# Attention and a channel mixture on one core: unsplit float32 scores for the first five head pairs, GpSimd casts in the early weight conversion, another PSUM half for early scores, a new order

## The chip, the cores and the metric

One core of a Trainium2 chip runs the whole program in one launch. The metric is device time in microseconds (us), lower is better. The profile names the engines PE (TensorE), DVE (VectorE), ACT (ScalarE), POOL (GpSimd) and SP (SyncE, which issues the DMAs).

## What is computed

```python
# q, k, v: (batch 8, heads 8, tokens 576, 64);  x: (8, 576, 512)
scores = q @ k^T / sqrt(64)
scores = where(scores >= max(scores) - tau, scores, -1e9)
attn   = exp(scores - max); attn /= sum(attn) + 1e-9
x      = attn @ v                       # heads side by side: 512 channels
theta  = x @ w_theta
zr, zi = x * cos(theta), x * sin(theta)
y      = w_tok_r @ zr + w_tok_i @ zi    # over the 576 tokens
u      = x + y
out    = u + max(u @ w_ch, 0)
```

## The kernel before, in words

Two heads form a pair; there are 32 pairs, four to a batch element. A pair n has five score units S n.0 to S n.4. A unit of the first four holds 128 query rows of both heads; the fifth holds the last 64 rows of both heads together. `unit` computes a unit's scores into four PSUM banks, DVE reads them out with a running minimum (the eviction, line 780), a small DVE instruction adds the threshold (790), ACT forms the masked exponentials in two passes per head (804, 811), and DVE transposes 32x32 blocks (823, 825). `values` multiplies the transposed weights by v (V n, line 840, in plain float32), and `divide` applies the row sums. When four pairs of a batch element are done, `mixture` does the rest for it: the theta products (T, line 948), sine and cosine on ACT, transposes on PE (1091), the token products (K, 1136) and the products with w_ch (T again).

Products that need more than one pass of the fast PE type (float32r) are split into a high word and a low word, and three products high-high, high-low, low-high are summed. For q and k this is done in `prepare_q` and `prepare_k`: load the raw tile, scale q by the gate (line 696; only from pair 3 on, since for pairs 0 to 2 the eviction multiplies by the gate instead), cast to the high word (705 and 722 on DVE, 707 and 724 on ACT), subtract to get the low word (`low`, line 530, on DVE or POOL).

The weights come as 64-bit floats. `convert` turns a chunk of them into a high and a low float32r word: ACT takes the magnitude (578), POOL or DVE clamps it (583), DVE shifts and merges bits (597, 604, 611), DVE multiplies the low 32 bits by a power of two (`word`, 615), ACT casts the high word (626), PE sums three terms (634 to 636; in the text, C) and ACT writes the low word (640). There are 17 chunks, called turns: 0 to 3 are w_theta (512 columns), 4 to 12 the token weights (576 columns, two C each), 13 to 16 w_ch. C0 to C21 belong to turns 0 to 12.

Nothing is scheduled at run time. The program lists its operations, and two tables decide the rest: `ORDER` says in which order they are issued (each engine works its own part in that order), and `PLACES` says in which buffer or PSUM bank each tile lies. All score units and all value products lie in banks 0 to 3 before the change (the digit 0 of a tile that is four banks wide); banks 4 to 7 serve the rest:

```python
ps = Buf(cl["bank"], lambda b: psum[:, b : b + 2 * len(heads)], psum=True,
         places=(0,) if i < 4 else (0, 2), wide=2 * len(heads))
terms = ((0, 0), (0, 1), (1, 0))
```

Of the kernel before, what the change touches and what calls it, by code (L numbers as in the profile page):

```python
# [64 lines left out]
        "0101201220220101200012012001201201201201022100121010210210012012011200"  # L65
    ),
    "xl": (
        "012102012001010231010120303120123201301230213012310230123301210232013102310232013"
    ),
    "xh": (  # L70
        "01203121013003013120120213201323010103210310230123210301230213012312030123102310231023102320131023"
    ),
    "rb": (
        "010101010001010101010000001000100000011101010100"
    ),
    "bank": (
        "67765674454565747576560000000070000007000000700000074567545744744475677457667547667576477675000000600000"
        "06000000600000056547646757456744754665674747677564570000005000000700000060000004765476576574567747655567"
        "74476545675600000040000007000000600000077564757467556437476556747564674775670000006000000600000070000006"
        "65745576564654776746554766575647745600000040000004000000600000047456567465556774564574677546754765760000"  # L80
        "00300000070000007000000576457675457467357456654767676476547600000060000006000000500005573273654727244354"
        "663726656457766453"
    ),
    "z": (
        "1201010212001200120012001200120012001200101"
    ),
    "rawq": (
        "01011100110010100101101010100010"
    ),
    "q": (  # L90
        "0123012301302103120312031203120312031203120312031201320123012301"
    ),
    "rawk": (
        "00000000000000000000000000000000"
    ),
    "k": (
        "0123012301230123012301230123012301230123012301230123012301230123"
# [5 lines left out]
        "10231032013201230132100231032101023031201230231202031012030112031021012020120123021032110213201230120310"  # L103
        "13202130012303102130120321103201203012302130023103201320120312231020123012313210103202103121032031023102"
        "31010230012301320132030123201301230130210230120301231123021031203121031321020310"
# [7 lines left out]
        "10120210010011201001001102100101002001102012011001001102"  # L113
    ),
    "rows": (
        "00100001001000101001010101000000"
    ),
    "a": (
        "00000000000000000000000000000000"
# [1193 lines left out]
```

## Time and profile before

| | |
|---|---|
| median of 3 runs | 926.42 us (924.15 to 927.21) |
| profiled execution | 924.78 us, of which the span from the first to the last instruction is 923.0 us |
| PE, DVE, ACT, POOL busy over the span | 866.0, 714.4, 699.5, 314.3 us |

PE is busy for most of the span, but its matmuls are pipelined and a busy time includes their fill, so the stretch matters more than the average. The span falls into an opening (up to the first score unit of pair 5, at 128.3 us), in which the five first pairs and the 13 first weight chunks are worked and hardly any mixture, and the rest, in which attention and mixture are interleaved.

### The profile page before, as it was taken

The page shows a single profiled execution, that of the slowest core. Times are in us where ns is not written, and L with a number is a line of the kernel's source. Part 1 is how long each engine was busy: PE and PEld are TensorE (multiplying, and loading weights), DVE is VectorE, ACT ScalarE, POOL GpSimd, SP SyncE. Part 2 cuts the span into 40 slices and gives each one's busy share as a digit, 9 for nine tenths or more (in the row PEclk, how much of TensorE's full clock was granted, in tenths as well). Part 3 has the DMA queues.
Part 4 walks back from the last instruction along what each step waited for, and adds up shares of the span by engine and source line. Part 5 has one row for each costly group of instructions (what it writes and reads, how often), then busy time and mean ns, then how long its engine had stood idle before and what let it go on. Part 6 is the DMA issues. An engine that isn't in the chain of part 4 may idle for free.

```text
span 923.0 us, 34024 instructions
## 1 busy us (share of the span) xinstructions
PE 866.0 (94%) x14632; PEld 779.5 (84%) x14632; DVE 714.4 (77%) x1598; ACT 699.5 (76%) x1406; POOL 314.3 (34%) x390
## 2 busy tenths in 40 slices
PE   4778799999999999999999999998999999999998
PEld 3556688788898988988999989897989989989898
DVE  7998889987787887778877887777975886876443
ACT  5788898865897678965899659976797659975540
POOL 0212451613443244513244343342334442321202
PEclk9988999999999999999999999999999999999999
DMA  7356535355342364024534351434534243423502
GB/s 261 115 161 224 166 138 178 101 167 178 131 158 93 131 209 175 17 80 151 201 103 144 110 187 67 170 107 143 183 129 129 82 146 122 138 83 131 164 22 75
DMA packets 62375, 126.15 MB, mean 137 GB/s; under 512 B 22512, under 2 KB 31632, under 8 KB 58128
## 3 DMA queue, kind: packets, MB, share of 16 engines
q1 hardware_dynamic: 62080, 123.97, 40.2%
q8 instruction: 115, 1.88, 0.8%
q14 instruction: 36, 0.29, 0.1%
q10 hardware_dynamic: 144, 0.00, 0.0%
HBM read 110.17 MB, written 13.78 MB: 134 GB/s over the span
## 4 chain that ended last, share of the span: by engine, by line
PE 64%; DVE 20%; ACT 8%; issue 3%; DMA 3%; POOL 1%; SPq 0%; DVEq 0%; POOLq 0%; ACTq 0%
PE banks_ps__66 L1136 21%; PE banks_ps__66 L840 14%; PE banks_ps__66 L948 13%; PE banks_ps__66 L759 11%; DVE sc L780 7%; DVE a L823 5%; PE banks_ps__66 L1091 3%; ACT sc L804 2%; ACT s L811 2%; DVE nm L790 1%; PE banks_ps__66 L634 1%; DMA z<-in_w_theta_dram 1%; DVE xl L530 1%; DVE z L1016 1%; DVE zl L1116 1%
## 5 line engine op out<-in xcount | busy, mean ns | idle before, releaser
L804 ACT ACTIVATE sc<-sc,nm 128x576 f32<-128x576 f32 x288 | 216.7, 771 | 78.6 <-DVE nm L790 75.1
L811 ACT ACTIVATE s<-sc,small 128x576 f32<-128x576 f32 x288 | 222.9, 775 | 5.1 <-DVE a L823 0.6
L823 DVE STREAM_TRANSPOSE a<-s 128x576 f32<-128x576 f32 x256 | 189.7, 759 | 35.3 <-PE banks_ps__66 L840 28.6
L759 PE MATMUL banks_ps__66<-k,q 64*128 64x288 f32 (+1 forms) x1728 | 178.7, 320 | 32.7 <-DVE sc L780 24.0
L780 DVE TENSOR_SCALAR_CACHE_REDUCE sc<-banks_ps__66 128x576 f32<-128x576 f32 x261 | 186.2, 741 | 13.2 <-PE banks_ps__66 L759 11.5
L759 PEld LDWEIGHTS banks_ps__66<-k,q 64*128 64x128 f32 (+1 forms) x1728 | 141.4, 194 | 61.1 <-DVE sc L780 37.9
L948 PE MATMUL banks_ps__66<-xh,wm 128*128 128x288 f32 x1024 | 168.9, 302 | 4.2 <-issue 1.6
L840 PE MATMUL banks_ps__66<-a,v 32*64 32x144 f32 x9216 | 165.0, 288 | 4.9 <-DVE sc L780 3.9
L1136 PE MATMUL banks_ps__66<-wt_h,zh 128*128 128x288 f32 x576 | 164.4, 309 | 1.7 <-DVE xT L1148 1.2
L840 PEld LDWEIGHTS banks_ps__66<-a,v 32*64 32x64 f32 x9216 | 146.9, 132 | 18.0 <-issue 9.2
L1136 PE MATMUL banks_ps__66<-wt_l,zh 128*128 128x288 f32 x576 | 160.6, 302 | 0.0
L948 PEld LDWEIGHTS banks_ps__66<-xh,wm 128*128 128x128 f32 x1024 | 143.4, 188 | 14.6 <-issue 8.6
L1066 POOL TENSOR_TENSOR z<-z,xT 128x288 f32<-128x288 f32 x112 | 91.7, 850 | 118.9 <-ACT z L1047 96.4
L1136 PEld LDWEIGHTS banks_ps__66<-wt_h,zh 128*128 128x128 f32 x576 | 108.9, 190 | 6.9 <-issue 3.9
L1136 PEld LDWEIGHTS banks_ps__66<-wt_l,zh 128*128 128x128 f32 x576 | 108.6, 189 | 2.8 <-issue 2.6
L530 POOL TENSOR_TENSOR k<-rawk,k 128x288 fp32r<-128x288 f32 x62 | 52.9, 860 | 168.5 <-DVE k L722 93.0
L530 POOL TENSOR_TENSOR xl<-xT,xh 128x288 fp32r<-128x288 f32 x78 | 66.8, 878 | 109.6 <-ACT xh L907 67.6
L1136 PE MATMUL banks_ps__66<-wt_h,zl 128*128 128x288 f32 x576 | 95.8, 301 | 0.0
L948 PE MATMUL banks_ps__66<-xl,wm 128*128 128x288 f32 x512 | 92.6, 300 | 2.9 <-issue 2.7
L1116 DVE TENSOR_TENSOR zl<-banks_ps__66,zh 128x512 fp32r<-128x512 f32 (+1 forms) x96 | 51.9, 547 | 56.1 <-ACT zh L1097 56.0
L1136 PEld LDWEIGHTS banks_ps__66<-wt_h,zl 128*128 128x128 f32 x576 | 81.5, 188 | 2.9 <-issue 2.4
L948 PEld LDWEIGHTS banks_ps__66<-xl,wm 128*128 128x128 f32 x512 | 75.0, 188 | 7.1 <-issue 6.0
(78 smaller groups left out, 996.3 us busy)
## 6 DMA issues: line engine op xcount, KB each, us to landing
v<-in_vp_dram SPq DMA_DIRECT2D x32, 1152.0 KB
wm<-wm_dram SPq DMA_DIRECT2D x64, 512.0 KB
rawq<-in_qT_dram SPq DMA_DIRECT2D x31, 320.0 KB
rawk<-in_kT_dram SPq DMA_DIRECT2D x31, 288.0 KB
out_dram<-xT SPq DMA_DIRECT2D x31, 288.0 KB
rb<-sums_dram SPq DMA_DIRECT2D x64, 128.0 KB
z<-in_w_tok_dram SPq DMA_DIRECT2D x9, 576.0 KB
wm_dram<-rb SPq DMA_DIRECT2D x16, 256.0 KB
```

The costliest lines, as they stand in the source:

```text
L530: eng.tensor_tensor(out=out()[:, c0:c1], in0=in0()[:, c0:c1], in1=in1()[:, c0:c1], op=ALU.subtract)
L759: nc.tensor.matmul(ps()[:, 2 * j + h, :HS], q[a]()[r, i * P : (i + 1) * P], k[c]()[r, h * HS : (h + 1) * HS], start=(x == 0), stop=(x == 2),)
L780: lambda j=j, sc=sc, scaled=scaled: nc.vector.tensor_scalar(out=sc().rearrange("p (a b) -> p a b", a=2), in0=ps()[:, 2 * j : 2 * j + 2, :H ...
L804: lambda j=j, sc=sc: nc.scalar.activation(out=sc(), in_=sc(), func=AF.Prelu, bias=nm()[:, 2 + j : 3 + j], scale=-1.0, alpha=STEEP),
L811: lambda j=j, sc=sc, total=total, weights=weights: nc.scalar.activation(out=weights(), in_=keys(sc()), func=AF.Exp, bias=back, accum_out=p ...
L823: nc.vector.transpose(out=a()[:, :, j, 32 * i : 32 * i + 32], in_=src.rearrange("p (c q) -> p c q", q=32))
L840: nc.tensor.matmul(ps()[64 * h : 64 * h + 64, b, :w], v()[r, c, h, :], a()[r, c, h, :], start=(c == 0), stop=(c == 17))
L948: nc.tensor.matmul(ps[h]()[:, :HS], wm()[:, a, c, :], parts[c][bb]()[:, h * HS : (h + 1) * HS], start=first and n == 0, stop=final and n = ...
L1066: eng.tensor_tensor(out=zi, in0=zi, in1=x[m]()[:, c0:c1], op=ALU.mult)
L1091: nc.tensor.transpose(out=tp()[:, i * P : (i + 1) * P], in_=z()[:, c : c + P], identity=ident)
L1116: lambda zh=zh, zl=zl, tv=tv: nc.vector.tensor_tensor(out=zl(), in0=tv(), in1=zh().bitcast(F32), op=ALU.subtract),
L1136: nc.tensor.matmul(ps()[:, :HS], zz[c][lo]()[:, zz[c][2]], w[:, c, hs], start=(q + n == 0), stop=(q + n == len(work) - 1),)
```

## The change

- For pairs 0 to 4 (`WHOLE = 5`) q and k are loaded straight into the tiles that PE reads, and the scores are one plain float32 product instead of three float32r products. No cast and no low word is made for them. POOL scales q of pairs 1 to 4 by the gate; pair 0 keeps the gate in its eviction.
- In `convert`, for turns 0 to 9 (`WORD_POOL = 10`) the low word is made on POOL by a cast of the low 32 bits and a multiplication, in halves; the power of two moves into the constant matrix `unit_low` of C. For turns 0 to 7 (`HI_POOL = 8`) POOL casts the high word instead of ACT.
- For pairs 0 to 4 (`TWICE = 5`) score units and value products may lie in banks 0 to 3 or in banks 4 to 7.
- `ORDER` and `PLACES` are new throughout.

```diff
+TWICE = 5
+WHOLE = 5
+HI_POOL = 8
+WORD_POOL = 10
-    one = const.tile([P, P], F32R, name="one")
-    nc.scalar.copy(out=one, in_=ident)
+    unit_low = const.tile([P, P], F32R, name="unit_low")
+    nc.scalar.mul(out=unit_low, in_=ident, mul=2.0**-52)
...
+        if turn < WORD_POOL:
+            for i in range(2):
+                r = slice(n * i // 2, n * (i + 1) // 2)
+                gps(
+                    c_pool(n // 2) * 0.6, lambda r=r: nc.gpsimd.tensor_copy(out=w()[:, r], in_=lb()[:, r]), key, (raw,),
+                    ((w, i),),
+                )
+                gps(
+                    c_pool(n // 2),
+                    lambda r=r: nc.gpsimd.tensor_tensor(
+                        out=w()[:, r], in0=w()[:, r].bitcast(F32), in1=mb()[:, r].bitcast(F32), op=ALU.mult
+                    ),
+                    key, ((w, i), mag), ((w, i),),
+                )
+        else:
...
+        if turn < HI_POOL:
+            gps(c_pool(n) * 0.5, lambda: nc.gpsimd.tensor_copy(out=hi(), in_=bb().bitcast(F32)), key, (bits,), (hi_b,), hold=hold)
+        else:
...
+        if n < WHOLE:
+            q = sb("q", [P, QS])
+            pr.q = (q, q)
...
+            if n:
+                gps(
+                    c_pool(QS) * 0.5, lambda: nc.gpsimd.tensor_scalar(out=q(), in0=q(), scalar1=gate, scalar2=None, op0=ALU.mult), key,
+                    ((q, 0), small_b), ((q, 0),),
+                )
+            return
...
-            cl["bank"], lambda b: psum[:, b : b + 2 * len(heads)], psum=True, places=(0,) if i < 4 else (0, 2), wide=2 * len(heads)
+            cl["bank"], lambda b: psum[:, b : b + 2 * len(heads)], psum=True,
+            places=((0, 4) if n < TWICE else (0,)) if i < 4 else (0, 2), wide=2 * len(heads),
...
-        terms = ((0, 0), (0, 1), (1, 0))
+        whole = n < WHOLE
+        terms = ((0, 0),) if whole else ((0, 0), (0, 1), (1, 0))
...
-            scaled = n >= AT["sq"]
+            scaled = n > 0
...
-        ps = Buf(cl["bank"], lambda b: psum[:, b : b + 4], psum=True, places=(0,), wide=4)
+        ps = Buf(cl["bank"], lambda b: psum[:, b : b + 4], psum=True, places=(0, 4) if n < TWICE else (0,), wide=4)
```

What the new order does is seen at three places. The first is the start of DVE's program, from the end of the constants on; k, q are the split words of the first pairs, rawk and rawq what was loaded, sc the evicted scores, nm their minimum. Before:

```order
L722 CAST k<-rawk 128x288
L705 CAST q<-rawq 128x128
L530 TENSOR_TENSOR q<-rawq,q 128x128
L530 TENSOR_TENSOR k<-rawk,k 128x288
L705 CAST q<-rawq 128x512
L530 TENSOR_TENSOR q<-rawq,q 128x512
L780 TENSOR_SCALAR sc,nm<-banks_ps__66,small 128x576 x2
L705 CAST q<-rawq 128x640
L790 TENSOR_SCALAR nm<-nm,small 128x2
L530 TENSOR_TENSOR q<-rawq,q 128x640
```

and of the change:

```order
L821 TENSOR_SCALAR sc,nm<-banks_ps__66,small 128x576 x2
L831 TENSOR_SCALAR nm<-nm,small 128x2
L821 TENSOR_SCALAR sc,nm<-banks_ps__66,small 128x576 x2
L831 TENSOR_SCALAR nm<-nm,small 128x2
L600 TENSOR_SCALAR xh<-xl 128x512
L607 SCALAR_TENSOR_TENSOR xh<-wm,xh 128x512
L864 STREAM_TRANSPOSE a<-s_116 128x18x32
L821 TENSOR_SCALAR sc,nm<-banks_ps__66,small 128x576
```

The casts and low words of pairs 0 and 1 are gone, evictions stand first, and the first weight chunk's bit work (L600, L607) stands behind the second eviction.

The second is POOL's program in the opening, where weight chunks (xl, xh, wm, z) and q of the next pairs meet. Before, from its first real work on:

```order
L530 TENSOR_TENSOR k<-rawk,k 128x288 x2
L583 TENSOR_SCALAR xl<-xl 128x256 x6
L583 TENSOR_SCALAR xl<-xl 128x288
L530 TENSOR_TENSOR k<-rawk,k 128x288 x2
L583 TENSOR_SCALAR xl<-xl 128x288
L530 TENSOR_TENSOR k<-rawk,k 128x288
```

and of the change, from the same place:

```order
L621 CAST xh<-wm 128x256
L586 TENSOR_SCALAR xl<-xl 128x256 x2
L640 CAST rb<-xh 128x512
L621 CAST xh<-wm 128x256
L626 TENSOR_TENSOR xh<-xh,xl 128x256 x2
L713 TENSOR_SCALAR q<-q,small 128x640
L586 TENSOR_SCALAR xl<-xl 128x256
L621 CAST xh<-wm 128x256
L586 TENSOR_SCALAR xl<-xl 128x256 x2
```

The low words of k are gone from POOL, and the casts and multiplications of the weights and the scaling of q stand between the clamps (L583 before, L586 now).

The third is PE's program at the end of the opening, where theta products of batch element 0 (xh and xl with wm) begin among the scores (k,q). Before, from unit S4.2 to unit S4.4 (S5.0 follows after 20 more theta matmuls):

```order
L759 MATMUL banks_ps__66<-k,q 128x288 x12
L948 MATMUL banks_ps__66<-xh,wm 128x288 x12
L948 MATMUL banks_ps__66<-xl,wm 128x288 x6
L759 MATMUL banks_ps__66<-k,q 128x288 x12
L948 MATMUL banks_ps__66<-xh,wm 128x288 x6
L948 MATMUL banks_ps__66<-xl,wm 128x288
L948 MATMUL banks_ps__66<-xh,wm 128x288 x2
L948 MATMUL banks_ps__66<-xl,wm 128x288
L948 MATMUL banks_ps__66<-xh,wm 128x288 x4
L948 MATMUL banks_ps__66<-xl,wm 128x288 x4
L948 MATMUL banks_ps__66<-xh,wm 128x288 x8
L759 MATMUL banks_ps__66<-k,q 128x288 x6
```

and of the change, from unit S4.4 to unit S5.0:

```order
L800 MATMUL banks_ps__66<-k,q 128x288 x2
L989 MATMUL banks_ps__66<-xh,wm 128x288 x12
L989 MATMUL banks_ps__66<-xl,wm 128x288 x6
L989 MATMUL banks_ps__66<-xh,wm 128x288 x6
L989 MATMUL banks_ps__66<-xl,wm 128x288
L989 MATMUL banks_ps__66<-xh,wm 128x288 x2
L989 MATMUL banks_ps__66<-xl,wm 128x288
L989 MATMUL banks_ps__66<-xh,wm 128x288 x8
L989 MATMUL banks_ps__66<-xl,wm 128x288 x4
L989 MATMUL banks_ps__66<-xh,wm 128x288 x4
L989 MATMUL banks_ps__66<-xl,wm 128x288 x4
L800 MATMUL banks_ps__66<-k,q 128x288 x12
```

All five units of pair 4 now stand ahead of the first theta product, and 48 theta matmuls stand ahead of S5.0 where 64 stood before. From S5.0 to S8.0 (the first unit of pair 8) PE has the same work in both, but for the 16 theta matmuls that moved behind S5.0 and eight w_ch matmuls that moved ahead of S8.0.

## Rows read from the trace of the kernel before

**Rows 1.** The page's first part: busy time of each engine over the span.

```profile
PE 866.0 (94%) x14632; PEld 779.5 (84%) x14632; DVE 714.4 (77%) x1598; ACT 699.5 (76%) x1406; POOL 314.3 (34%) x390
```

**Rows 2.** Windows: stretch, length, busy us per engine (instructions), granted clock, DMA share, GB/s.

```profile
7.60:128.30 120.70, 94.06 (x1593) 75.28 (x1594) 109.24 (x240) 100.78 (x213) 34.61 (x52) 0.93 0.57 189
128.30:212.70 84.40, 79.67 (x1354) 69.25 (x1354) 73.16 (x157) 69.52 (x135) 32.17 (x36) 1.00 0.47 147
212.70:845.70 633.00, 618.40 (x10893) 563.70 (x10892) 495.27 (x1121) 499.90 (x1007) 236.91 (x284) 1.00 0.39 130
```

**Rows 3.** Waits from 0 to 128.3 us: who waited for whom, total, times, longest.

```profile
PE banks_ps__66 L759 <- DVE sc L780: 20.1, 16, 2.5
...
DVE sc L780 <- PE banks_ps__66 L759: 6.6, 11, 1.2
```

**Rows 4.** Timeline of PE: start, length, line, operation, tiles, count, idle before it.

```profile
9.23 1.81 PE L759 MATMUL banks_ps__66<-k,q 64*128 64x288 f32 x12 [1.66 <-DVE sc L780]
...
29.47 4.48 PE L840 MATMUL banks_ps__66<-a,v 32*64 32x144 f32 x144 [1.66 <-DVE sc L780]
...
35.41 2.51 PE L840 MATMUL banks_ps__66<-a,v 32*64 32x144 f32 x144
38.99 1.07 PE L759 MATMUL banks_ps__66<-k,q 64*128 64x288 f32 x12 [1.07 <-ACT xT L856]
```

**Rows 5.** DVE by line and form, 0 to 128.3 us: count, busy us, mean ns, idle.

```profile
L780 DVE TENSOR_SCALAR_CACHE_REDUCE sc<-banks_ps__66,small 128x576 f32<-128x576 f32 x27 | 21.0, 810 | 4.7 <-PE banks_ps__66 L759 4.5
L780 DVE TENSOR_SCALAR_CACHE_REDUCE sc<-banks_ps__66 128x576 f32<-128x576 f32 x18 | 12.9, 748 | 2.4 <-PE banks_ps__66 L759 2.0 <-ACT wt_l L640 0.2
L615 DVE SCALAR_TENSOR_TENSOR xh<-z,xl 128x576 fp32r<-128x576 uint32 x9 | 6.7, 755 | 0.1
L530 DVE TENSOR_TENSOR q<-rawq,q 128x640 fp32r<-128x640 f32 x3 | 2.5, 817 | 0.0
L696 DVE TENSOR_SCALAR rawq<-rawq,small 128x640 f32<-128x640 f32 x4 | 2.2, 548 | 0.0
L705 DVE CAST q<-rawq 128x640 fp32r<-128x640 f32 x3 | 1.5, 489 | 0.0
L615 DVE SCALAR_TENSOR_TENSOR xh<-wm,xl 128x512 fp32r<-128x512 uint32 x2 | 1.4, 688 | 0.0
L722 DVE CAST k<-rawk 128x576 fp32r<-128x576 f32 x3 | 1.4, 462 | 0.6 <-DMA rawk<-in_kT_dram 0.6
```

**Rows 6.** Timeline of all engines: the first and last of pair 0's eight preparing DVE instructions.

```profile
4.56 0.30 DVE L722 CAST k<-rawk 128x288 fp32r<-128x288 f32 x1
...
6.78 0.69 DVE L530 TENSOR_TENSOR q<-rawq,q 128x512 fp32r<-128x512 f32 x1
```

**Rows 7.** ACT by line and form, 0 to 130 us.

```profile
L626 ACT CAST wt_h<-xh 128x576 fp32r<-128x576 f32 x9 | 6.0, 664 | 2.9 <-DVE xh L604 2.9
L626 ACT CAST rb<-xh 128x512 fp32r<-128x512 f32 x4 | 2.4, 607 | 2.6 <-DVE xh L604 2.6
L707 ACT CAST q<-rawq 128x640 fp32r<-128x640 f32 x3 | 2.2, 725 | 0.0
```

**Rows 8.** POOL by line and form, 0 to 130 us.

```profile
L530 POOL TENSOR_TENSOR k<-rawk,k 128x288 fp32r<-128x288 f32 x10 | 8.7, 878 | 28.9 <-DVE k L722 12.0 <-ACT k L724 8.5 <-PE banks_ps__66 L840 8.4
L583 POOL TENSOR_SCALAR xl<-xl 128x288 f32<-128x288 f32 x18 | 8.4, 482 | 31.2 <-ACT xl L578 17.4 <-DMA rb<-sums_dram 9.9 <-issue 4.0
L530 POOL TENSOR_TENSOR q<-rawq,q 128x320 fp32r<-128x320 f32 x6 | 5.7, 965 | 5.8 <-PE banks_ps__66 L759 5.8
```

**Rows 9.** DVE's small instruction by form, 0 to 128.3 us.

```profile
L790 DVE TENSOR_SCALAR nm<-nm,small 128x2 f32<-128x2 f32 x20 | 5.6, 279 | 0.2
L790 DVE TENSOR_SCALAR nm<-nm,small 128x1 f32<-128x1 f32 x5 | 0.9, 187 | 0.1
```

**Rows 10.** Timeline: first theta products on PE; the eviction of S5.0 on DVE.

```profile
114.63 1.87 PE L948 MATMUL banks_ps__66<-xh,wm 128*128 128x288 f32 x12
...
128.34 0.71 DVE L780 TENSOR_SCALAR_CACHE_REDUCE sc<-banks_ps__66 128x576 f32<-128x576 f32 x1
```

More of the change, by code (lines that the diff above doesn't have):

```diff
@@ L121 @@
     "xT": (
-        "01234560321405632140536410253461"
+        "01234560231450623145026431524063"
     ),
@@ L634, in sum_up @@
                 nc.tensor.matmul(t, ident, bb().bitcast(F32)[:, r], start=True, stop=False)
-                nc.tensor.matmul(t, one, w()[:, r], start=False, stop=False)
+                nc.tensor.matmul(t, unit_low, w()[:, r], start=False, stop=False)
                 nc.tensor.matmul(t, minus, hi()[:, r], start=False, stop=True)
@@ L686, in prepare_q @@
         pr = pairs[n]
+        if n < WHOLE:
+            q = sb("q", [P, QS])
+            pr.q = (q, q)
+            for i, (c0, c1) in enumerate(pieces_q(n)):
+                load(
+                    lambda r=slice(c0, c1): nc.sync.dma_start(q()[:, r], qT[n // NP, n % NP][:, r]),
+                    (key if n else -95.0 + 4 * i) + A("raw", n), (), ((q, i),), (c1 - c0) // 2,
+                )
[3 more added lines that the diff above has]
+                    ((q, 0), small_b), ((q, 0),),
+                )
+            return
         raw = sb("rawq", [P, QS])
@@ L714, in prepare_k @@
         pr = pairs[n]
+        if n < WHOLE:
+            k = sb("k", [P, S])
+            pr.k = (k, k)
+            for i, (c0, c1) in enumerate(pieces_k(n)):
+                load(
+                    lambda r=slice(c0, c1): nc.sync.dma_start(k()[:, r], kT[n // NP, n % NP][:, r]),
+                    (key if n else -96.0 + 2 * i) + A("raw", n), (), ((k, i),), (c1 - c0) // 2,
+                )
+            return
         raw = sb("rawk", [P, S])
@@ L760, in score @@
                             ps()[:, 2 * j + h, :HS], q[a]()[r, i * P : (i + 1) * P], k[c]()[r, h * HS : (h + 1) * HS],
-                            start=(x == 0), stop=(x == 2),
+                            start=(x == 0), stop=(x == len(terms) - 1),
                         )
-        pe(
-            6 * c_mm(HS), score, t0 + A("score", n), [
-                *((q[0], c) for c, (c0, _) in enumerate(pieces_q(n)) if c0 <= i * P),
-                *((q[1], [(c, d) for d in range(AT["cut"])]) for c, (c0, _) in enumerate(pieces_q(n)) if c0 <= i * P),
-                k[0], k[1],
-            ],
-            ((ps, list(heads)),),
-            12 * len(heads), mode="r" if i < 4 else "m",
+        pieces = [c for c, (c0, _) in enumerate(pieces_q(n)) if c0 <= i * P]
+        if whole:
+            R = [*((q[0], c) for c in pieces), k[0]]
+        else:
+            R = [*((q[0], c) for c in pieces), *((q[1], [(c, d) for d in range(AT["cut"])]) for c in pieces), k[0], k[1]]
+        pe(
+            0.97 if whole else 6 * c_mm(HS), score, t0 + A("score", n), R, ((ps, list(heads)),),
+            (8 if whole else 12) * len(heads), mode="r" if i < 4 else "m",
         )
```

82 lines of the change are left out of this document (39 added, 43 removed), and 260 rows, old and new, of the table ORDER.

## The prediction

> **What bounds the kernel now.** I read the page's totals first. PE is busy for 866.0 of 923.0 us [rows 1], so at most 57 us of the span is free of it, and a change pays only where PE is not already full. The windows view says where that is; I cut it at three evictions, those of S5.0, S8.0 and S31.4 [rows 2]. From 212.7 to 845.7 us PE is busy for 618.4 of 633.0 us, 98%: the steady state belongs to PE, and nothing in this change takes work from PE there. From 128.3 to 212.7 it is 79.7 of 84.4 us, 94%. In the opening, from 7.6 to 128.3 us, it is 94.1 of 120.7 us, 78%, while DVE is busy for 109.2 us (91%) and ACT for 100.8 (83%). So DVE sets the pace of the opening, ACT stands close behind, and POOL, at 34.6 us (29%), has room.
>
> The waits of the opening show the second limit [rows 3]: PE waited 20.1 us in 16 places for DVE's evictions, and DVE waited 6.6 us in 11 places for PE's scores. That is a ping-pong over one set of four banks: PE can't write the next unit before DVE has emptied the last one, and DVE has nothing to evict while PE writes. At 29.47 us a value product waits for an eviction in the same way [rows 4].
>
> The timeline also shows PE's clock. The 12 matmuls of a unit took 1.81 us at 9.23 and 1.07 us at 38.99, the same 144 value matmuls 4.48 us at 29.47 and 2.51 at 35.41 [rows 4]. That is the lower level (1.2 GHz) up to about 34 us and the upper (2.4 GHz) behind it; over the rest of the opening the mean granted clock is 0.93 [rows 2], so the lower level came back a few times.
>
> **What the change removes from DVE.** I sum up to the eviction of S5.0, at 128.34 us before [rows 10]; all of these instructions stand ahead of it in both orders.
> - Pair 0's eight casts and low words run from 4.56 to 7.47 us [rows 6], ahead of the first eviction. Without them PE can start when q and k have landed, but its first unit is four passes long instead of three. I give this 0.3 us, between 0 and 2.9.
> - Pairs 1 to 4: two q casts at 0.489, three low words of q at 0.817, two k casts at 0.462, two scalings at 0.548 [rows 5]: 0.98 + 2.45 + 0.92 + 1.10 = 5.4 us.
> - `word` for turns 0 to 9: six of 576 columns at 0.755 and four of 512 at 0.688 [rows 5]: 7.3 us.
> - The 18 evictions of pairs 1 and 2 no longer read the gate: 0.810 against 0.748 [rows 5], 1.1 us.
>
> Together 13.8 us behind the first eviction. Records of neighbouring DVE instructions overlap at their ends, so I take 13.0. The order also leaves about 0.7 us of mixture work for behind S5.0.
>
> **ACT** loses eight high-word casts, four at 0.664 and four at 0.607 [rows 7], and the q and k casts of pairs 2 and 3 (two at 0.725, two of the shape of the 0.664 row): 5.1 + 2.8 = 7.9 us. About 93 of its 100.8 us stay, which fits into the shorter opening. So this costs and gains nothing by itself; it only keeps ACT from becoming the next limit.
>
> **POOL** loses eight low words of k at 0.878 and two of q at 0.965 [rows 8], 9.0 us. It gains 20 half-chunk casts, 20 half-chunk multiplications, eight whole-chunk casts and four scalings of q (640 columns). A multiplication has two inputs, like the 0.878 row. A cast or a scaling has one input, like the clamp at 0.482 for 288 columns [rows 8]; no row shows a cast on POOL, here one from 32-bit integers that lie eight bytes apart. Call the price of a half-chunk cast x: the bounds are 0.48 (the clamp) and 0.88 (a two-input instruction), with nothing above them shown. With whole chunks at 2x, scalings at 2.2x, multiplications at 16.8 us together, the 26 clamps of 13 turns at 12 and the rest at 5, POOL has 45x + 34 us to do: 56 us at the lower bound, 74 at the upper, in about 106. It is nearest to the lower row (one input), and it is not the limit at either. The work that hides it is the opening itself: if one of these lands late, PE waits at its C with the scores queued behind it.
>
> **PE** gains a little. A value product shows plain float32: 72 products of 144 columns, eight side by side, in 2.51 us, so about 0.25 us for 144 columns and 1.0 us for a unit's two halves; with the fill of some 0.35 us (1.07 less six passes of 0.12) a unit takes 1.3 us at the upper level and 2.3 at the lower [rows 4], 0.24 and 0.48 us more than now. For 25 units, about half at each level, that is 9 us of PE time, under DVE's cover as long as PE has its 26 us of idle time in the opening.
>
> **The banks.** With two sets, PE writes one unit while DVE empties the other. Of the 6.6 us that DVE waited for PE I take half, 3.3 us, as gained; between 0 and 6.6.
>
> **What it costs.** DVE's small instruction averages 0.279 us on two columns and 0.187 on one [rows 9]; one column more doesn't explain that, and time in which POOL held it may. Twenty of these differences are 1.8 us. With POOL's share about doubled I charge 2.0 us more for DVE instructions held up by POOL, between 0 and 6. For new waits of PE or DVE on POOL's casts I charge 1.0 us.
>
> The Trainium skill, GPSIMD Engine Reference, "Key points", says that GpSimd shares its SBUF interfaces with VectorE and contends with DVE instructions that run in a two-port mode or have two SBUF inputs; that speaks against moving work to POOL, and its own result is the third rival below. Section "Engine selection" of the same page calls one-input work on GpSimd roughly line-rate, which fits the lower bound of x; no run here shows that for these casts.
>
> **The sum.** S5.0's eviction comes at 128.3 - 0.3 - 13.0 - 0.7 - 3.3 + 2.0 + 1.0 = 114.0 us, 14.3 earlier. Behind it PE is the limit, with the same work but for 16 theta matmuls that now stand behind S5.0: twelve took 1.87 us [rows 10], so 16 cost 2.5. The rest of the order changes nothing that I can price; PE's 97% from 128.3 us on leaves it little either way, and I allow 3 us both ways. The profiled execution of 924.78 us becomes 924.8 - 14.3 + 2.5 = 913.0. It lies 1.6 us under the median of the runs, so the median should be 914.6.
>
> **The rivals.**
> 1. *POOL becomes the limit of the opening* (the one that ends on the slower side). If a cast from strided integers costs far more than any row suggests, the C of the weight chunks wait on POOL; in the new PE order C8 to C11 stand ahead of S3.4, so the scores wait as well. The opening would end when POOL's 45x + 34 us, begun at about 9 us, are done. The gain is gone when that is at 125.8 us (128.3 less the 2.5 of the moved matmuls), x = 1.84 us; from x = 1.9 on it is slower by more than 0.3%, at x = 2.1 the median is 938. Short of that, x = 1.6 gives an opening of 115 us and no loss, but uneven waits that I put at 5 us, 919 to 920. For it: the price isn't shown, and the chains are long. Against it: the one-input row is a quarter of that. Chance 0.13, of which 0.07 slower.
> 2. *PE becomes the limit of the opening.* Its 94.1 us plus 9 less 2.5 are 100.6 of 106 us if the clock stays as it is; that is 95%, and PE can't have that in an order with evictions between. At 88% busy S5.0 comes at 122 and the median is 922.6; at 92% it is 117 and 917.6. For it: the lower clock level up to 34 us. Against it: the busy time counts fill, and a denser PE got the upper level everywhere else [rows 2]. Chance 0.13; I put its time at 920.
> 3. *Contention eats the relief.* Some 70 DVE instructions of the opening are casts, bit operations and small ones; if each is held for 0.1 us more, as the two forms in [rows 9] differ, that is 7 us in place of 2, and the median is 919 to 920. Chance 0.12.
> 4. *More than I think.* All of the 6.6 us go, nothing waits on POOL, and the first 34 us run at the upper clock level: 5 us more, 906 to 910. Chance 0.10.
> 5. *The new order gives it back*: the steady state loses what the opening gains, 922 to 930. Nothing in the rows speaks for it but that every position changed. Chance 0.06.
>
> The forecast, 910 to 918, has 0.46. The range of 8 in 10 reaches from 907 to 925. A measurement of this kernel tells about 0.3% (2.8 us) from no change. Faster by more than that: the forecast and rivals 2 to 4 (0.81), most of the milder part of 1 (0.04 of 0.06) and half of 5 (0.03), 0.88. Within it the rest of these, 0.05; slower the hard part of 1, 0.07.
>
> **What would show each step.** In the changed profile: the eviction of S5.0 at about 114 us, between 110 and 120; S8.0 some 87 us later, and from there to the end 710 us as before. DVE's busy time in the opening near 97 us and ACT's near 93; the waits of DVE on scores (line 821 on line 800) halved or less. POOL's cast near 0.5 us a half chunk, its share of the opening near 55%. A float32 unit at 1.3 us, or 2.3 at the lower clock level. The small DVE instruction (line 831) no longer than 0.35 us on average. The prediction is wrong if POOL's casts take over 1.5 us, if PE's wait for POOL at the C shows up among the longest waits, if S5.0 comes after 120 us, or if the steady stretch from S8.0 on is longer by more than 3 us.

## The result and the profile after

The changed kernel's median is 910.89 us (909.44 to 914.24, 4 runs), against 926.82 us (924.15 to 927.38, 4 runs) for the kernel before beside it: ratio 0.9839, 95% interval 0.9806 to 0.9872, 15.9 us faster. The forecast was 914.6. The profiled execution took 910.66 us, of which the span is 908.9.

The page's first part, as [rows 1]:

```profile
PE 860.7 (95%) x14542; PEld 771.0 (85%) x14542; DVE 714.4 (79%) x1571; ACT 692.2 (76%) x1394; POOL 341.0 (38%) x432
```

Over the span DVE is as busy as before, 714.4 us to the tenth, although instructions priced at 13.8 us were taken off it. Where the time went shows only in the stretches. The windows view of the changed kernel, cut at the same three evictions as [rows 2] (the first row is the opening from its first eviction, the second the same from 7 us on, the third lies inside it):

```profile
6.90:112.90 106.00, 86.09 (x1480) 63.04 (x1479) 103.46 (x220) 92.19 (x196) 64.47 (x94) 0.94 0.60 200
7.00:112.90 105.90, 85.99 (x1480) 62.96 (x1477) 103.36 (x220) 92.19 (x196) 64.47 (x94) 0.94 0.60 200
9.50:33.70 24.20, 17.57 (x340) 11.65 (x336) 23.60 (x55) 21.45 (x44) 14.54 (x21) 0.86 0.57 210
112.90:197.70 84.80, 83.27 (x1389) 74.12 (x1388) 72.69 (x159) 70.74 (x141) 30.11 (x36) 1.00 0.47 154
197.70:832.20 634.50, 618.18 (x10891) 563.22 (x10891) 503.29 (x1122) 500.32 (x1007) 235.74 (x284) 1.00 0.39 132
832.20:908.90 76.70, 70.80 (x780) 68.83 (x778) 33.98 (x66) 27.35 (x53) 10.01 (x12) 1.00 0.25 87
```

and two rows of the same view of the kernel before, for the comparison with the second and third:

```profile
7.00:128.30 121.30, 94.62 (x1599) 75.50 (x1596) 109.71 (x241) 100.78 (x213) 34.61 (x52) 0.93 0.57 189
9.50:33.70 24.20, 16.02 (x210) 13.24 (x210) 20.87 (x50) 17.86 (x34) 3.98 (x8) 1.00 0.55 206
```

The opening is 15.4 us shorter. In it DVE's busy time falls by only 6.4 us, from 109.7 to 103.4; its idle time, the length of the stretch less the busy time, falls by 9.1, from 11.6 to 2.5. DVE is busy for 98% of the opening. Behind it almost nothing changed: 84.8 us for 84.4, then 634.5 for 633.0, then 76.7 for 77.3. DVE's busy time grew there, 503.3 for 495.3 us in the steady stretch, where PE is busy for 97% of the time and DVE for 79%; the stretch is 1.5 us longer.

The waits of the opening, as [rows 3] (waiting engine, what it waited for: total, times, longest):

```profile
PE banks_ps__66 L800 <- DVE sc L821: 8.1, 4, 3.3
...
PE banks_ps__66 L881 <- DVE a L866: 4.1, 1, 4.1
DVE sc L821 <- PE banks_ps__66 L800: 3.2, 4, 2.4
```

The wait of PE's score units for evictions went from 20.1 us in 16 places to 8.1 in 4 (C waits for evictions as well now, 2.7 us in 3 places), and DVE's wait for scores from 6.6 in 11 to 3.2 in 4, of which 2.4 are the very first eviction.

PE's timeline, as [rows 4] (a unit of four products of two heads is eight matmuls now; the first row covers four units with their waits):

```profile
4.56 7.07 PE L800 MATMUL banks_ps__66<-k,q 64*128 64x288 f32 x32 [4.56 <-DMA q<-in_qT_dram]
13.11 1.24 PE L800 MATMUL banks_ps__66<-k,q 128*128 128x288 f32 x4 [1.49 <-DVE sc L821]
16.89 1.24 PE L800 MATMUL banks_ps__66<-k,q 64*128 64x288 f32 x8 [1.06 <-POOL q L713]
21.44 2.29 PE L800 MATMUL banks_ps__66<-k,q 64*128 64x288 f32 x8 [3.31 <-DVE sc L821]
27.23 1.24 PE L800 MATMUL banks_ps__66<-k,q 64*128 64x288 f32 x8
```

and a row of the windows view for the unit that begins at 21.44:

```profile
21.00:24.00 3.00, 2.56 (x23) 1.53 (x31) 2.74 (x7) 3.00 (x8) 0.52 (x2) 0.50 0.06 20
```

A float32 unit takes 1.24 us at the upper clock level (2.4 GHz) and 2.29 at the lower (1.2 GHz). The upper level is there at 13 us; behind PE's idle 3.31 us the unit at 21.44 ran at the lower one, with a granted clock of 0.50. Before, units took the time of the lower level up to about 34 us.

DVE by line and form in the opening, as [rows 5] and [rows 9] (busy us, mean ns, idle in front):

```profile
L864 DVE STREAM_TRANSPOSE a<-s 128x576 f32<-128x576 f32 x39 | 28.4, 754 | 0.0
L821 DVE TENSOR_SCALAR_CACHE_REDUCE sc<-banks_ps__66 128x576 f32<-128x576 f32 x36 | 25.9, 738 | 1.1 <-PE banks_ps__66 L800 0.8 <-ACT s L852 0.3
L831 DVE TENSOR_SCALAR nm<-nm,small 128x2 f32<-128x2 f32 x20 | 8.0, 401 | 0.4
L607 DVE SCALAR_TENSOR_TENSOR xh<-z,xh 128x576 uint32<-128x576 uint32 x9 | 7.6, 840 | 0.1
...
L614 DVE TENSOR_SCALAR xl<-xh 128x512 uint32<-128x512 uint32 x4 | 2.8, 706 | 0.1
L607 DVE SCALAR_TENSOR_TENSOR xh<-z,xh 128x512 uint32<-128x512 uint32 x2 | 2.3, 1143 | 0.1
```

and of the kernel before, the rows that answer to the last three of these:

```profile
L604 DVE SCALAR_TENSOR_TENSOR xh<-z,xh 128x576 uint32<-128x576 uint32 x9 | 6.7, 749 | 0.0
...
L611 DVE TENSOR_SCALAR xl<-xh 128x512 uint32<-128x512 uint32 x4 | 1.6, 420 | 0.0
...
L604 DVE SCALAR_TENSOR_TENSOR xh<-z,xh 128x512 uint32<-128x512 uint32 x2 | 1.4, 684 | 0.0
```

Unchanged instructions became longer: the small one from 279 to 401 ns, the merges from 749 to 840 and from 684 to 1143, the shift at 512 columns from 420 to 706. Evictions and transposes did not (738 for 748, 754 for 763).

POOL by line and form in the opening, as [rows 8]:

```profile
L626 POOL TENSOR_TENSOR xh<-xh,xl 128x288 fp32r<-128x288 f32 x12 | 10.2, 858 | 7.6 <-DVE xl L614 7.0 <-DVE nm L831 0.5
...
L713 POOL TENSOR_SCALAR q<-q,small 128x640 f32<-128x640 f32 x4 | 7.7, 1923 | 0.0
...
L621 POOL CAST xh<-z 128x288 fp32r<-128x288 uint32 x12 | 5.9, 495 | 1.8 <-PE banks_ps__66 L651 1.6 <-PE banks_ps__66 L650 0.2
...
L640 POOL CAST wt_h<-xh 128x576 fp32r<-128x576 f32 x4 | 3.7, 914 | 0.0
```

### The profile page after: what moved, and what is told of

Read it like the earlier page. It is cut to its first block, busy times and chain, and to the rows that moved or that the text cites. A ratio compares the mean times of both kernels' runs of the same rounds, so it can differ in the third digit from the quotient of the medians.

```text
span 908.9 us, 33820 instructions
## 1 busy us (share of the span) xinstructions
PE 860.7 (95%) x14542; PEld 771.0 (85%) x14542; DVE 714.4 (79%) x1571; ACT 692.2 (76%) x1394; POOL 341.0 (38%) x432
## 4 chain that ended last, share of the span: by engine, by line
PE 62%; DVE 23%; ACT 7%; issue 4%; DMA 2%; POOL 1%; SPq 1%; DVEq 0%; POOLq 0%; ACTq 0%
PE banks_ps__66 L1177 20%; PE banks_ps__66 L989 14%; PE banks_ps__66 L881 13%; PE banks_ps__66 L800 10%; DVE sc L821 8%; DVE a L864 4%; PE banks_ps__66 L1132 3%; ACT s L852 2%; ACT sc L845 2%; DVE nm L831 2%; DVE xl L533 1%; DVE xh L607 1%; DVE a L866 1%; ACT ang L1023 1%; PE banks_ps__66 L650 1%
## 5 line engine op out<-in xcount | busy, mean ns | idle before, releaser
L821 DVE TENSOR_SCALAR_CACHE_REDUCE sc<-banks_ps__66 128x576 f32<-128x576 f32 x279 | 199.7, 743 | 13.2 <-PE banks_ps__66 L800 11.6
L864 DVE STREAM_TRANSPOSE a<-s 128x576 f32<-128x576 f32 x256 | 187.3, 758 | 26.4 <-PE banks_ps__66 L881 18.9
L800 PE MATMUL banks_ps__66<-k,q 64*128 64x288 f32 (+1 forms) x1638 | 176.6, 326 | 17.4 <-DVE sc L821 11.7
L881 PE MATMUL banks_ps__66<-a,v 32*64 32x144 f32 x9216 | 168.6, 288 | 12.8 <-issue 7.1
L989 PE MATMUL banks_ps__66<-xh,wm 128*128 128x288 f32 x1024 | 171.9, 304 | 3.7 <-issue 1.4
L800 PEld LDWEIGHTS banks_ps__66<-k,q 64*128 64x128 f32 (+1 forms) x1638 | 134.0, 188 | 45.6 <-DVE sc L821 22.6
L881 PEld LDWEIGHTS banks_ps__66<-a,v 32*64 32x64 f32 x9216 | 148.4, 132 | 27.2 <-issue 15.9
L1177 PE MATMUL banks_ps__66<-wt_h,zh 128*128 128x288 f32 x576 | 160.8, 304 | 0.9 <-ACT zh L1138 0.8
L1107 POOL TENSOR_TENSOR z<-z,xT 128x288 f32<-128x288 f32 x112 | 89.3, 832 | 100.8 <-ACT z L1088 100.8
L533 POOL TENSOR_TENSOR k<-rawk,k 128x288 fp32r<-128x288 f32 x54 | 47.5, 890 | 139.4 <-ACT k L763 69.8
L533 POOL TENSOR_TENSOR q<-rawq,q 128x320 fp32r<-128x320 f32 x54 | 48.2, 906 | 97.9 <-ACT q L737 44.6
```

What stands on the lines that cost most here:

```text
L533: eng.tensor_tensor(out=out()[:, c0:c1], in0=in0()[:, c0:c1], in1=in1()[:, c0:c1], op=ALU.subtract)
L800: nc.tensor.matmul(ps()[:, 2 * j + h, :HS], q[a]()[r, i * P : (i + 1) * P], k[c]()[r, h * HS : (h + 1) * HS], start=(x == 0), stop=(x == l ...
L821: lambda j=j, sc=sc, scaled=scaled: nc.vector.tensor_scalar(out=sc().rearrange("p (a b) -> p a b", a=2), in0=ps()[:, 2 * j : 2 * j + 2, :H ...
L864: nc.vector.transpose(out=a()[:, :, j, 32 * i : 32 * i + 32], in_=src.rearrange("p (c q) -> p c q", q=32))
L881: nc.tensor.matmul(ps()[64 * h : 64 * h + 64, b, :w], v()[r, c, h, :], a()[r, c, h, :], start=(c == 0), stop=(c == 17))
L989: nc.tensor.matmul(ps[h]()[:, :HS], wm()[:, a, c, :], parts[c][bb]()[:, h * HS : (h + 1) * HS], start=first and n == 0, stop=final and n = ...
```

## The experiments

The result leaves two readings. By the sum in the prediction, work taken off DVE shortens the opening nearly one for one, whatever the order. The rival reading is that DVE's waits decide, and that the parts are worth something only in an order that fits them. So the parts were put into the kernel before one by one and together, with its own order, and the placements on POOL were taken out of the changed kernel one by one. The new order without the unsplit scores, without the second set of banks, or without any of the parts was not run. All runs are compared with the kernel before on the same chip. S5.0, busy and idle time are those of each kernel's one profiled execution; the last column of the table is DVE's wait for scores from the start of the program on.

| kernel before, its order, with | ratio, 95% interval | S5.0 at | DVE busy, from 7 us to S5.0 | DVE idle there | waits for PE's scores |
|---|---|---|---|---|---|
| nothing | 1 | 128.3 | 109.7 | 11.6 | 6.6 |
| unsplit scores | 1.0028 (1.0005 to 1.0051) | 134.0 | 104.3 | 22.7 | 15.1 |
| PSUM halves | 0.9904 (0.9882 to 0.9927) | 124.2 | 110.0 | 7.2 | 3.0 |
| words on POOL | 1.0068 (1.0050 to 1.0087) | 134.4 | 108.2 | 19.2 | 7.7 |
| scores and halves | 0.9953 (0.9921 to 0.9985) | 124.9 | 104.4 | 13.5 | 6.9 |
| words and halves | 1.0042 (1.0017 to 1.0066) | 131.9 | 108.2 | 16.7 | 4.7 |
| scores and words | 1.0063 (1.0040 to 1.0086) | 136.8 | 103.0 | 26.8 | 14.9 |
| all three | 1.0005 (0.9984 to 1.0026) | 130.2 | 102.9 | 20.3 | 8.3 |
| the changed kernel | 0.9839 (0.9806 to 0.9872) | 112.9 | 103.4 | 2.5 | 3.2 |

**Unsplit scores alone.** The places of the dropped casts in the program stay empty:

```diff
-        raw = sb("rawq", [P, QS])
-        q1, q2 = pr.q = [sb("q", [P, QS], F32R) for _ in range(2)]
+        whole = n < 5
+        raw = sb("q" if whole else "rawq", [P, QS])
+        q1, q2 = pr.q = (raw, raw) if whole else [sb("q", [P, QS], F32R) for _ in range(2)]
...
-        terms = ((0, 0), (0, 1), (1, 0))
+        terms = ((0, 0),) if n < 5 else ((0, 0), (0, 1), (1, 0))
```

> The kernel before with its order and banks, and only the unsplit float32 scores of pairs 0 to 4 (their casts and low words are left out of the program). Theory (DVE's work is the limit of the opening): DVE loses 5.4 us of casts and low words behind the first eviction, less what overlaps, so 4 to 5 us faster, 922. Rival (the ping-pong over one set of banks is the limit): a unit is 0.24 to 0.48 us longer on PE and nothing hides it, so not faster, 0 to 5 us slower. Rival (the new order gives the gain): no change within 1 us.

It measured 930.38 us, 1.0028: slightly slower. Its row of the windows view for the opening, and the first rows of DVE's waits there:

```profile
7.00:134.00 127.00, 102.86 (x1505) 73.62 (x1506) 104.28 (x233) 99.11 (x209) 24.65 (x42) 0.92 0.53 176
```

```profile
DVE sc L791 <- PE banks_ps__66 L771: 15.1, 12, 2.2
DVE xh L920 <- PE banks_ps__66 L634: 2.9, 1, 2.9
```

DVE has 5.4 us less to do (the prediction counts 4.4 for the casts and low words of pairs 1 to 4; the end of pair 0's lies behind 7 us too; the scalings stay) and idles 11.1 us more. PE's busy time rose by 8.2 us, close to the 9 us of the prediction: a longer unit, at the old clock levels, over one set of banks, makes DVE wait longer for each. So this run takes work off DVE and gives PE more at the same time; it does not show what the relief of DVE would be worth by itself.

**PSUM halves alone.** Only the table of banks is new; among the early units and value products ten switch to the other half, as many as the old order leaves room for.

> The kernel before with its order, and only other banks: units and value products of pairs 0 to 2 lie in either half of PSUM as far as the old order leaves room (ten switches of half among the first twelve of these tiles). Theory: DVE's waits for scores in the first 40 us shrink; 2 us faster, 3.3 at most. Rival (ping-pong is the limit): 6 us faster or more. Rival (the order): no change.

It measured 919.93 us, 0.9904, some 9 us faster, well past the forecast of the term. Its row of the opening:

```profile
7.00:124.20 117.20, 94.08 (x1599) 75.39 (x1596) 109.95 (x241) 101.20 (x213) 35.14 (x52) 0.93 0.59 195
```

S5.0 comes 4.1 us earlier, DVE's idle time goes from 11.6 to 7.2 us, PE's wait for evictions from 20.1 to 11.7. Its profiled execution is at the upper end of its runs (922.37 of 917.64 to 923.34), so its rows may understate the gain; where the rest of the 9 us lies, the trace does not show.

**Words on POOL alone.** As in the change, the power of two moves into the constant of C.

```diff
+            def word_pool():
+                for i in range(2):
+                    r = slice(n * i // 2, n * (i + 1) // 2)
+                    nc.gpsimd.tensor_copy(out=w()[:, r], in_=lb()[:, r])
...
+                    nc.gpsimd.tensor_tensor(out=w()[:, r], in0=w()[:, r].bitcast(F32), in1=mb()[:, r].bitcast(F32), op=ALU.mult)
-            dve(c_two(n), lambda: word(nc.vector), key, (raw, mag), (w,), lock=True)
+            dve(c_two(n), word_pool if turn < 10 else lambda: word(nc.vector), key, (raw, mag), (w,), lock=True)
-        act(c_act(n), lambda: nc.scalar.copy(out=hi(), in_=bb().bitcast(F32)), key, (bits,), (hi_b,), hold)
+        high = nc.gpsimd.tensor_copy if turn < 8 else nc.scalar.copy
+        act(c_act(n), lambda: high(out=hi(), in_=bb().bitcast(F32)), key, (bits,), (hi_b,), hold)
```

> The kernel before with its order, and only the weight conversion changed: low words of ten chunks and high words of eight on POOL. Theory: DVE loses 7.3 us and pays some 2 to 3 us for what POOL holds up, so 4 to 5 us faster. Rival (contention eats the relief): DVE's small instructions and bit operations grow by as much as was removed, no change or slower. Rival (the order): no change, or slower, since POOL's casts come late for C in the old order.

It measured 935.56 us, 1.0068: slower. The ten words were 7.3 us of DVE, but its busy time fell by 1.5 us; of the other 5.8 some 5 are found in longer instructions, while POOL's busy time went from 34.6 to 65.7. And DVE now stood waiting for a clamp queued behind the new casts, a row of its waits:

```profile
DVE xh L597 <- POOL xl L583: 7.9, 3, 3.0
```

**All three in the old order.**

> The kernel before with its order, and all three: float32 scores, either half of PSUM as far as the old order leaves room, casts and low words on POOL. What is left to the changed kernel is its new order (and the scaling of q on POOL). Theory: 9 to 12 us faster, so that the order is worth 4 to 7. Rival (the order is the gain): 4 us faster at most, the order worth 12. Rival (sum of parts): as much as the three single runs together.

It measured 928.02 us, 1.0005, no change. The row of its opening:

```profile
7.00:130.20 123.20, 97.87 (x1505) 69.31 (x1502) 102.91 (x224) 95.07 (x201) 55.13 (x90) 0.88 0.55 182
```

The first of DVE's waits:

```profile
DVE sc L795 <- PE banks_ps__66 L775: 8.3, 6, 2.2
DVE xh L592 <- POOL xl L578: 5.5, 2, 2.8
DVE a L838 <- PE banks_ps__66 L855: 3.4, 2, 2.2
```

DVE's busy time, 102.9 us, is that of the changed kernel, 103.4. The opening is 17.3 us longer all the same, and all of that is idle time of DVE: 20.3 us against 2.5. DVE's waits name PE's scores with 8.3 us, POOL's clamps with 5.5 and PE's value products with 3.4. Two things limit this reading. The profiled execution (932.45 us) is the slowest of this kernel's 12, 4.4 us above the median; by the medians the changed kernel is some 15 to 17 us faster than this one, in all. And PE is busy for 97.9 us here and 86.0 in the changed kernel: 2.5 of that are the 16 theta matmuls, the rest goes with a granted clock of 0.88 against 0.94. How much of the waiting on PE comes from the order itself and how much from the clock that came with it was not separated.

**The pairs of parts**, which tell whether one part's wait hides in another's:

> The kernel before, its order, with two parts: the unsplit float32 scores of pairs 0 to 4 and the other PSUM halves (the same ten switches as in the run with the halves alone). Alone the scores measured 1.0028 of before, the halves 0.9904. Theory A (each part's worth in this order adds to the others'): 0.9932, about 920.5 us. Theory B (the scores lost because the longer float32 units alternate with DVE's evictions over one set of banks, and a second set frees the DVE work that they save): the loss goes and some of the 5.4 us of removed DVE work shows, 0.984 to 0.990, 912 to 918 us; DVE's idle time on PE in the opening then falls from 15 us to under 8.

> The kernel before, its order, with two parts: the low and high weight words on POOL and the other PSUM halves. Alone the words measured 1.0068, the halves 0.9904. Theory A (worths add): 0.9972, about 924 us. Theory B (DVE waits in this order for what POOL finishes late, and a second set of banks can't help that): all of the loss stays and part of the halves' gain goes as well, 0.998 to 1.004. If it is 0.993 or less, the loss was a wait over the banks and not POOL.

> The kernel before, its order, with two parts: the unsplit scores and the weight words on POOL; one set of banks as before. Alone 1.0028 and 1.0068. Theory A (worths add): 1.0096, about 935 us. Theory B (both losses are DVE standing idle, on PE in the one, on POOL in the other, so that one wait covers part of the other): 1.003 to 1.007, 929 to 933 us. Faster than before only if the removed DVE work needs both parts to show, which nothing so far suggests.

Scores with halves came to 0.9953: the halves take back 9 of the 11 us of waiting that the longer units made, but no more, so the 5.4 us of removed work still don't show. That is near the plain sum of the two alone, 0.9932, which lies in the interval. Words with halves came to 1.0042, where the sum of the two would be 0.9972: the wait for POOL's clamps stayed at 7.9 us, which a second set of banks did not touch, and most of the halves' gain went as well. Scores with words came to 1.0063, below the sum of 1.0096: the two waits cover each other in part. In no pair did S5.0 come earlier than in the same kernel without the part that takes work off DVE.

**Words back on DVE in the changed kernel.** Its order stays; POOL's casts and multiplications are replaced by DVE's one instruction.

```diff
-                    c_pool(n // 2) * 0.6, lambda r=r: nc.gpsimd.tensor_copy(out=w()[:, r], in_=lb()[:, r]), key, (raw,),
+                    c_pool(n // 2) * 0.6, lambda: None, key, (raw,),
...
-                    lambda r=r: nc.gpsimd.tensor_tensor(
-                        out=w()[:, r], in0=w()[:, r].bitcast(F32), in1=mb()[:, r].bitcast(F32), op=ALU.mult
+                    lambda i=i: i and nc.vector.scalar_tensor_tensor(
+                        out=w()[:, :n], in0=lb(), scalar=1.0, in1=mb().bitcast(F32), op0=ALU.mult, op1=ALU.mult
```

> The changed kernel with its order, and the low words of turns 0 to 9 back on DVE, one instruction each. Theory (DVE is still the limit of the opening, 103.5 of 106.0 us busy): DVE gets 7.3 us back and loses the contention of 40 POOL instructions (some 3 us), so 4 us slower than the changed kernel, 915. Rival (DVE's relief does not matter, the banks and the order do): as the changed kernel, 911. Rival (contention costs as much as the words): as the changed kernel, with DVE's small instruction back near 0.28 us.

It measured 929.57 us, 1.0034: the whole gain is gone, far more than any of the three expectations gave. S5.0 came at 130.1 us.

```profile
7.00:130.10 123.10, 92.01 (x1481) 65.80 (x1478) 105.02 (x231) 92.46 (x196) 40.27 (x54) 0.88 0.52 173
```

DVE's busy time is only 1.7 us above the changed kernel's (105.0: the words came back, and most of the contention went), but it idled for 18.1 us. Two rows of PE's waits:

```profile
PE banks_ps__66 L651 <- DVE xh L626: 9.2, 4, 5.4
PE banks_ps__66 L800 <- DVE sc L821: 8.2, 4, 4.8
```

DVE makes the words late, PE waits for them at C with scores queued behind, and DVE then waits for those scores (9.9 us in 7 places). This is the mirror of the run with all three parts: the new order without this placement brings no gain, and neither do all three parts in the old order. PE also waited 5.1 us once for a k that landed late. Here DVE's instruction stands where the order put POOL's multiplications; whether the words could stand on DVE at a better place in it was not tried.

**High words back on ACT; q scaled by ACT; the gate back in the evictions.** Three small edits of the changed kernel:

```diff
-            gps(c_pool(n) * 0.5, lambda: nc.gpsimd.tensor_copy(out=hi(), in_=bb().bitcast(F32)), key, (bits,), (hi_b,), hold=hold)
+            gps(c_pool(n) * 0.5, lambda: nc.scalar.copy(out=hi(), in_=bb().bitcast(F32)), key, (bits,), (hi_b,), hold=hold)
```

> The changed kernel with its order, and the high words of turns 0 to 7 back on ACT. Theory: ACT goes from 92.2 to 97.3 us in the opening and is not the limit, POOL loses 6.4 us, so within 1.5 us of the changed kernel. Rival (ACT stands so close behind DVE that it becomes the limit): 3 to 5 us slower.

```diff
-                    c_pool(QS) * 0.5, lambda: nc.gpsimd.tensor_scalar(out=q(), in0=q(), scalar1=gate, scalar2=None, op0=ALU.mult), key,
+                    c_pool(QS) * 0.5, lambda: nc.scalar.activation(out=q(), in_=q(), func=AF.Copy, scale=gate), key,
```

> The changed kernel with its order, and q of pairs 1 to 4 scaled on ACT instead of POOL, where it takes 1.92 us each. Theory: POOL loses 7.7 us, ACT gains 2.9, and DVE's instructions are held up less; 0 to 2 us faster than the changed kernel. Rival (ACT becomes the limit, or PE waits for ACT's turn): 2 us slower.

```diff
-                    c_pool(QS) * 0.5, lambda: nc.gpsimd.tensor_scalar(out=q(), in0=q(), scalar1=gate, scalar2=None, op0=ALU.mult), key,
+                    c_pool(QS) * 0.5, lambda: None, key,
...
-            scaled = n > 0
+            scaled = n >= WHOLE
```

> The changed kernel, with the gate of pairs 1 to 4 multiplied in at the evictions, as before for the first pairs, and the four scalings of q on POOL (1.92 us each) taken out. 36 evictions are about 0.06 us longer, 2.2 us more for DVE; POOL has 7.7 us less to do. Theory A (DVE at 98% sets the opening's length, and 25 us less of POOL gave it 4.2 us back, so 7.7 give about 1.3): 0 to 2 us slower than the changed kernel, 0.983 to 0.986. Rival (the scaling stands on the way to the scores of pair 1, which waited 1.1 us for it, and is late as when ACT does it): 2 to 4 us faster, 0.979 to 0.982.

They measured 914.41 us (0.9856, interval 0.9828 to 0.9884), 916.04 us (0.9876, 0.9852 to 0.9900) and 913.23 us (0.9838, 0.9799 to 0.9876). All three intervals overlap that of the changed kernel (0.9806 to 0.9872), so none is told apart from it for certain; the scaling on ACT, with PE waiting 3.9 us for one late q, may cost a few us. DVE's idle time stays at 4.4, 5.9 and 3.6 us. So these placements are not what the gain hangs on. The last kernel also shows that POOL's scaling of q, which the run with all three parts lacks, does not explain the difference between that run and the changed kernel.

**The low words of the first ten chunks left out** in the changed kernel (C adds the high word in their place, so this part of the weights' conversion is not computed): 40 POOL instructions fewer.

```diff
-                    c_pool(n // 2) * 0.6, lambda r=r: nc.gpsimd.tensor_copy(out=w()[:, r], in_=lb()[:, r]), key, (raw,),
+                    c_pool(n // 2) * 0.6, lambda: None, key, (raw,),
...
-                nc.tensor.matmul(t, unit_low, w()[:, r], start=False, stop=False)
+                nc.tensor.matmul(t, unit_low, (hi()[:, r] if turn < WORD_POOL else w()[:, r]), start=False, stop=False)
```

> The changed kernel with its order, and no low word made for turns 0 to 9: POOL's 20 casts and 20 multiplications are left out, and PE multiplies the high word by the same tiny matrix instead, so that part of the low word of these weights is left out of the result. Theory (contention with POOL costs DVE 4 to 6 us of the opening): DVE's busy time in the opening falls from 103.5 to about 99, its small instruction from 0.40 us to about 0.30, and the time by 3 to 5 us against the changed kernel. Rival (what DVE loses to POOL is hidden elsewhere): within 1 us of the changed kernel.

Its row of the opening, and three of DVE's rows by form there:

```profile
7.00:110.00 103.00, 85.21 (x1481) 62.58 (x1478) 99.25 (x221) 92.22 (x196) 39.36 (x54) 0.95 0.61 206
```

```profile
L607 DVE SCALAR_TENSOR_TENSOR xh<-z,xh 128x576 uint32<-128x576 uint32 x9 | 6.8, 755 | 0.1
...
L614 DVE TENSOR_SCALAR xl<-xh 128x512 uint32<-128x512 uint32 x4 | 1.7, 425 | 0.1
...
L607 DVE SCALAR_TENSOR_TENSOR xh<-z,xh 128x512 uint32<-128x512 uint32 x2 | 1.4, 696 | 0.1
```

With POOL's busy time down from 64.5 to 39.4 us the merges and the shift at 512 columns are back at the durations of before (755, 696 and 425 ns), DVE's busy time is 4.1 us less, and S5.0 comes 2.9 us earlier in this profiled execution, the fastest of the five. Two forms did not come back: the small instruction took 368 ns on average (expected was about 300, before it was 279), and the shift at 576 columns 581 (598 in the changed kernel, 454 before).

The timelines tell why. Two small instructions of the changed kernel, the first with POOL at rest, the second beside two of POOL's casts:

```profile
10.37 0.23 DVE L831 TENSOR_SCALAR nm<-nm,small 128x2 f32<-128x2 f32 x1
...
44.05 0.43 POOL L621 CAST xh<-z 128x288 fp32r<-128x288 uint32 x1
...
44.40 0.66 DVE L831 TENSOR_SCALAR nm<-nm,small 128x2 f32<-128x2 f32 x1
44.43 0.61 POOL L640 CAST rb<-xh 128x512 fp32r<-128x512 f32 x1
```

The second ends with the cast. Of the 20 small instructions on two columns, 6 meet no work of POOL in the changed kernel and take 0.17 to 0.23 us; the 14 that meet some average 0.49. Before, 14 meet none (0.18 to 0.23) and 6 do (0.43). Without the words it is 12 (0.17 to 0.23) and 8 (0.60): scalings and additions of POOL still meet them. So the contention is shown, instruction by instruction, and what is left of it to gain is small: the median, 911.82 us (0.9820, 0.9790 to 0.9849), can't be told from the changed kernel's.

## Why the prediction was right, and where it was not

**The bound and the place.** Right. All of the gain came in the opening; S5.0 came at 112.9 us (forecast 114.0), S8.0 84.8 us later (87), and from there to the end it took 711.2 us (710). The 16 theta matmuls that moved were charged 2.5 us behind S5.0; the three stretches there grew by 0.4, 1.5 and -0.6, together 1.3.

**The sum was right by two errors that cancel.** Its terms against the trace, as changes of the opening in us:

| term | forecast | measured |
|---|---|---|
| first eviction earlier | -0.3 | -0.7 (6.9 for 7.6) |
| DVE busy: removed work, order, contention (-13.0 - 0.7 + 2.0) | -11.7 | -5.8 (109.24 to 103.46) |
| DVE idle: banks, new waits (-3.3 + 1.0) | -2.3 | -8.9 (11.46 to 2.54) |
| S5.0 | -14.3 | -15.4 |

The first failed term is the contention, "I charge 2.0 us more for DVE instructions held up by POOL": it measured nearly 8. The instructions that both kernels have and that grew add up to 8.3 us: the small one 20 x (401 - 279) ns = 2.4 (the prediction allowed it 350 ns), the merges 2.3, the shifts 2.4, the rest 1.2. That is why DVE's busy time is 103.5 and not 97. The run with only the words on POOL shows some 5 us by itself. Rival 3 had this mechanism with 7 us, so its size was right, and it missed the time because the idle time fell as well.

The second is the idle time. The prediction took it as nearly fixed, half of DVE's 6.6 us of waiting for scores, and let removed work show one for one. The runs in the old order show that neither holds. There the work that DVE lost came back as waiting for PE or POOL; with all three parts its idle time is 20.3 us. No run takes work off DVE without giving PE or POOL more, so what the relief alone would be worth stays open. For the order in the opening the prediction had no term but the 0.7 us of moved work, and that is the larger part: with equal busy time of DVE, the idle time is 17.8 us less with the new order, its buffers and the clock that came with them. So the place and the total were right, and the total by luck. Which of the moved instructions do it wasn't separated, and one set of banks or split scores in the new order weren't tried.

**PE and the clock.** The price of a float32 unit, 1.3 and 2.3 us, was right (1.24 and 2.29), and so were the 9 us of PE time as long as the clock stays as it was (8.2 measured with the unsplit scores alone). The reading of the clock in the prediction needs a correction: 0.93 is the mean of the whole opening [rows 2], not of the part behind 34 us. In the changed kernel units ran at the upper level from about 13 us on rather than 34, with the relapse shown above, the part of rival 4 that happened: PE's 172 + 20 early score matmuls, S5.0 included, took 36.4 us, no more than the 37.1 of the split ones. So rival 2, PE at 100.6 of 106 us, did not come: it was 86.0.

**POOL.** The half-chunk cast at 0.495 us was near the lower bound as chosen, and rival 1 with its 1.84 us was far off. The scaling of q was priced at 2.2x, about 1.06 us, and took 1.92. POOL was busy for 61% of the opening (forecast 55%). Most of that miss is a slip in the sum: of the 34.6 us of before, less the 9.0 that go and 12 of clamps, 13.6 remain and not "the rest at 5"; the trace shows about 14. The sum is then 45x + 43, and rival 1 would have had no gain left from x = 1.64 on instead of 1.84, still far from 0.495. PE's waits for it were 1.6 us, 1.1 for the first scaled q and 0.5 at C, where 1.0 was charged. The Trainium skill, GPSIMD Engine Reference, "Engine selection", calls one-input work there roughly line-rate. In this case a cast of 576 columns took 914 ns on POOL for DVE's 462 [rows 5], and the scaling 1923 for 548: the scaling does not agree with it, and the cast took twice DVE's time.

**Which instructions the contention reaches.** After the rows above: the Trainium skill, GPSIMD Engine Reference, "Key points", has GpSimd contend with DVE instructions that have two SBUF inputs or run in a two-port mode. The merges (two SBUF inputs, 749 to 840 ns and back to 755 without POOL's words) and the evictions from PSUM (748 to 738) agree with it. The shift (420 to 706, and back to 425) and the small instruction (279 to 401) have one input; whether they run in such a mode no run here shows. How often the two engines meet counts as much as how busy POOL is: with only the words on POOL the merges stayed at 744 ns while the other shift, at 576 columns, went from 530 to 650.

## What to carry to other kernels

Where two engines hand work to each other through one set of buffers, work saved on one can turn into idle time: count that idle time, and ask which wait ends it. A change of placement and a change of order have to be judged together; here all three parts in the old order measured no change, the new order without the words on POOL 0.3% slower, and both together 1.6% faster. When a forecast of a sum comes true, compare its terms as well: busy and idle time apart showed two errors of about 6 us each that the total hid.

## What was not expected of the hardware

- A small DVE instruction of some 0.2 us took up to 0.97 us beside work of POOL, and the one shown above ended within 0.02 us of POOL's cast.
- POOL's scaling of 640 float32 columns by a value read from SBUF took 1923 ns, four times a clamp of 288 columns (482 ns), while its cast of 576 columns took 914.
- Moving ten instructions of DVE (7.3 us) to POOL lowered its busy time by only 1.5 us in the old order, so that four fifths of the relief never arrived; in the new order, taking that POOL work away gave DVE 4.1 us back.
- The granted clock column read 1.00 for the kernel before from 9.5 to 33.7 us, where its score units took 1.81 us and more against 1.07 later. For the changed kernel it read 0.86 in the same window, and there it agrees with the durations: one of the four units shown above took 2.29 us. So the column did not show the lower level of the kernel before in this stretch; the durations of equal matmuls did.
